# RWKV6 attention and a tanh-shrink layer on one core: the first layer's products joined by three feature tiles instead of two

## The chip, the cores and the metric

The kernel runs on one core of a Trainium2 chip. Four engines matter: TensorE (PE, with its weight loads as PEld), VectorE (DVE), ScalarE (ACT) and SyncE (SP), which issues the transfers from and to device memory. The metric is the time of one execution on the device in microseconds (us). Everything is float32 at the interface; the products of the two layers are made in float32.

## The reference

```python
def _attn_ref(r, k, v, w, u):
    B, H, S, D = r.shape                      # 4, 8, 768, 48
    state = np.zeros((B, H, D, D))
    for t in range(S):
        cur = np.einsum('bhd,bhe->bhde', u[None] * kt, vt)
        y[:, :, t] = np.einsum('bhd,bhde->bhe', rt, state + cur)
        state = wt[:, :, :, None] * state + np.einsum('bhd,bhe->bhde', kt, vt)
...
x = attn_out.transpose(0, 2, 1, 3).reshape(B * S, H * D)   # 3072 x 384
h = x @ w_in                                               # w_in 384 x 2048
g = h - np.tanh(h)
return g @ w_out                                           # w_out 2048 x 384
```

A recurrent attention over 768 steps for 4 batches and 8 heads, whose result, as 3072 tokens of 384 features, goes through two dense layers with g = h - tanh(h) between them.

## The kernel before, in words

**Blocks.** The 3072 tokens are cut into 8 blocks of NB = 384 tokens (a batch's first or second half). For a block the first layer makes 16 feature tiles, each of 128 features by 384 tokens; w_in lies in on-chip memory as `w_in_sb[:, f, k]`, 16 by 3 squares of 128x128. While the two layers of block i run, the attention of block i+1 is worked on piece by piece, and what can be prepared of block i+2. The names of these pieces in code: `earlier` (scores between chunks, products at L508, masked into place by VectorE at L516), `split` and `join` (ScalarE's copies at L556 and L566 that prepare a transposition by DMA, `turned`), `update` (new states: products L589, VectorE's chain L601), `results` (products L785, ScalarE's copies L757 into the next block's tokens `xT`), `bound` (ScalarE's sums over 780 columns, L474). VectorE's own share of them is called `times_behind`, `before`, `held`, `product_u` and the like.

**The first layer.** A tile that stands alone takes three products of 384 columns (`first`, L899), added up in the PSUM bank `hp`. In blocks 2 to 7 some tiles are taken two at a time instead (class `Twos`, from L909): the tokens are cut in two halves of HB = 192, and of the 12 half-size products that two tiles need, a fast matrix product (Winograd's form of Strassen's) leaves 11. It needs sums and differences of squares of w_in (`weight_forms`, L937, made once by VectorE and kept in `kept`), of halves of the tokens (`token_forms`, L945, four per block), and of the results (`begin`): ScalarE copies one product from PSUM to `joint` (L962), and VectorE adds the other six PSUM regions to it in four instructions (L971). Products that only have to be added are added by TensorE in PSUM. Which tiles are joined stands in `JOINED` (L125): three pairs in block 2, six in blocks 3 to 6, seven in block 7; the other tiles stand alone.

**Between the layers.** `slight` (L977) makes g of a tile: two Tanh of different scale on ScalarE (L987, L988), a Square with an accumulated sum (L991) by which the kernel later sees whether the approximation held, and on VectorE the product of the two times a constant (L905).

**The second layer.** `Fewer` takes two tiles of g at a time as 128x128 squares and makes 15 products for 18 (`product`, L1096, 128 columns each) after a fast product too. Its forms of w_out are made in block 1 (L1354), its forms of g by VectorE for every pair (`form_g`, L1010), its 15 running sums over the eight pairs lie in four PSUM regions; products 12 to 14 (`others`, L1124) have a region at times that is shared with the first layer's `hp` or the attention's scratch. At a block's end ScalarE scales the sums out of PSUM (L1109) and VectorE combines them (L1132) into the output.

**The order.** All of it is written in the order in which each engine is to run it. The main loop goes over tiles f of a block; `plan(i)` says which attention piece stands at which tile; the long chain of `if joined ... elif` decides in which order VectorE's instructions of one tile stand, and `between(a, b)` deals two lists alternately, so that an instruction seldom stands directly behind the one whose result it needs. `due` holds second-layer products until two tiles later. PSUM has eight banks: three of `acc`, `hp`, and two pairs of scratch (`att`), which pairs of tiles, attention products and transpositions share in turn. Idle instructions (`empty`) are put in at some blocks' starts to shift code.

## Time and profile before

| | |
|---|---|
| median of 3 runs | 536.88 us (536.12, 536.88, 1406.05) |
| the profiled execution | 535.64 us |
| its span (first to last instruction) | 533.9 us |
| granted TensorE clock, mean | 0.999 |
| instructions | 14969 |
| read from device memory / written | 44.73 MB / 4.72 MB |

The span is what the trace covers; the time of the execution is a little longer. Busy time is the time in which an engine executes. On VectorE and ScalarE the next instruction starts a little before the one ahead has ended, so a row's duration is more than the distance between two starts. A matrix product in float32 shows as two records in the trace. One block of blocks 2 to 6 takes some 62 us.

### The profile page before, as it was taken

The page shows a single profiled execution, that of the slowest core. Times are in us where ns is not written, and L with a number is a line of the kernel's source. Part 1 is how long each engine was busy: PE and PEld are TensorE (multiplying, and loading weights), DVE is VectorE, ACT ScalarE, POOL GpSimd, SP SyncE. Part 2 cuts the span into 40 slices and gives each one's busy share as a digit, 9 for nine tenths or more (in the row PEclk, how much of TensorE's full clock was granted, in tenths as well). Part 3 has the DMA queues.
Part 4 walks back from the last instruction along what each step waited for, and adds up shares of the span by engine and source line. Part 5 has one row for each costly group of instructions (what it writes and reads, how often), then busy time and mean ns, then how long its engine had stood idle before and what let it go on. Part 6 is the DMA issues. An engine that isn't in the chain of part 4 may idle for free.

```text
span 533.9 us, 14969 instructions
## 1 busy us (share of the span) xinstructions
PE 523.9 (98%) x6040; PEld 449.2 (84%) x6040; DVE 478.1 (90%) x1011; ACT 312.4 (59%) x729; POOL 9.1 (2%) x57
## 2 busy tenths in 40 slices
PE   7999999999999999999999999999999999999996
PEld 5756665677887879999799998999889997999994
DVE  7999996698889999999999999999999999667874
ACT  4999984665536473655646375375735655454350
POOL 1100000000000000000000000000000000000001
PEclk9999999999999999999999999999999999999999
DMA  8799632352312452035420832145321430200011
GB/s 282 258 406 342 224 120 71 107 132 64 122 26 72 104 143 95 0 89 166 120 58 2 192 119 66 54 66 142 108 88 31 79 116 1 58 1 1 10 36 48
DMA packets 53048, 56.35 MB, mean 106 GB/s; under 512 B 21488, under 2 KB 50928, under 8 KB 52976
## 3 DMA queue, kind: packets, MB, share of 16 engines
q1 hardware_dynamic: 52592, 55.18, 34.7%
q8 instruction: 49, 0.80, 0.6%
q14 instruction: 23, 0.19, 0.1%
q10 hardware_dynamic: 288, 0.10, 0.1%
q0 software_dynamic: 96, 0.07, 0.1%
HBM read 44.73 MB, written 4.72 MB: 93 GB/s over the span
## 4 chain that ended last, share of the span: by engine, by line
PE 83%; DVE 13%; issue 2%; DMA 1%; SPq 0%; DVEq 0%
PE acc L1096 23%; PE att L961 20%; PE hp L899 17%; PE acc L1047 6%; PE hp L1096 5%; PE att L785 3%; DVE g L1010 2%; PE att L508 2%; DVE joint L971 2%; DVE g L905 1%; PE att L589 1%; DVE pre L431 1%; PE acc L1074 1%; PE att L1096 1%; PE att L899 1%
## 5 line engine op out<-in xcount | busy, mean ns | idle before, releaser
L1096 PE MATMUL acc<-forms,g 128*128 128x128 f32 x972 | 135.5, 276 | 0.0
L1096 PEld LDWEIGHTS acc<-forms,g 128*128 128x128 f32 x972 | 124.3, 192 | 3.8
L899 PE MATMUL hp<-xT,w_sb 128*128 128x384 f32 x330 | 116.5, 489 | 0.0
L1010 DVE TENSOR_TENSOR g<-g 128x256 f32<-128x256 f32 x270 | 110.5, 418 | 6.1 <-DVE g L1010 0.5
L899 PEld LDWEIGHTS hp<-xT,w_sb 128*128 128x128 f32 x330 | 59.5, 190 | 33.3
L905 DVE SCALAR_TENSOR_TENSOR g<-h,qa 128x384 f32<-128x384 f32 x112 | 61.7, 551 | 18.1 <-ACT h L991 17.9
L987 ACT ACTIVATE h<-joint 128x384 f32<-128x384 f32 x54 | 27.9, 517 | 77.5 <-DVE joint L971 77.5
L961 PE MATMUL att<-xT,w_sb 128*128 128x192 f32 x340 | 72.0, 326 | 0.0
L987 ACT ACTIVATE h<-hp 128x384 f32<-128x384 f32 x55 | 27.2, 495 | 58.5 <-PE hp L899 58.4
L991 ACT ACTIVATE h<-h 128x384 f32<-128x384 f32 x113 | 58.2, 515 | 0.0
L961 PEld LDWEIGHTS att<-xT,w_sb 128*128 128x128 f32 x340 | 56.4, 190 | 0.0
L971 DVE TENSOR_TENSOR joint<-joint,att 128x384 f32<-128x384 f32 (+1 forms) x108 | 51.6, 499 | 4.9 <-PE att L961 3.0
L1096 PE MATMUL acc<-w_sb,g 128*128 128x128 f32 x324 | 54.5, 277 | 0.0
L1096 PEld LDWEIGHTS acc<-w_sb,g 128*128 128x128 f32 x324 | 45.9, 192 | 4.4
L961 PE MATMUL att<-turned,kept 128*128 128x192 f32 x192 | 36.5, 327 | 0.1
L1132 DVE TENSOR_TENSOR sums<-sums 128x256 f32<-128x256 f32 x84 | 33.3, 410 | 1.4 <-ACT sums L1109 0.9
L1047 PE MATMUL acc<-w_sb,sums 128*128 128x384 f32 x96 | 33.7, 487 | 0.0
L272 ACT ACTIVATE up<-raw 128x768 f16<-128x768 f32 (+1 forms) x32 | 33.0, 1108 | 0.0
L961 PEld LDWEIGHTS att<-turned,kept 128*128 128x128 f32 x192 | 32.0, 190 | 0.4 <-DVE turned L945 0.4
L1096 PE MATMUL hp<-w_sb,g 128*128 128x128 f32 x176 | 29.5, 275 | 0.0
L1047 PEld LDWEIGHTS acc<-w_sb,sums 128*128 128x128 f32 x96 | 18.1, 190 | 12.3
L988 ACT ACTIVATE qa<-joint 128x384 f32<-128x384 f32 x54 | 27.5, 509 | 0.0
(157 smaller groups left out, 795.5 us busy)
## 6 DMA issues: line engine op xcount, KB each, us to landing
raw<-in_weights SPq DMA_DIRECT2D x16, 768.0 KB, 7.4
w<-in_wT SPq DMA_DIRECT2D x7, 780.0 KB, 4.4
k<-in_kT SPq DMA_DIRECT2D x7, 768.0 KB, 4.6
r<-in_rT SPq DMA_DIRECT2D x7, 768.0 KB, 4.5
v_sb<-in_v SPq DMA_DIRECT2D x8, 576.0 KB, 5.1
k<-in_tokens SPq DMA_DIRECT2D x7, 576.0 KB, 4.1
r<-in_tokens SPq DMA_DIRECT2D x7, 576.0 KB, 4.2
out_y<-sums SPq DMA_DIRECT2D x18, 128.0 KB, 1.9
```

Source lines behind the costliest of these rows:

```text
L272: return lambda: nc.scalar.activation(out=to, in_=of, func=AF.Copy, scale=scale, bias=bias)
L899: nc.tensor.matmul(hp, lhsT=w_in_sb[:, f, kc, :], rhs=xT[kc], start=(kc == KC - 1), stop=(kc == 0))
L905: return lambda: nc.vector.scalar_tensor_tensor(out=out, in0=in0, scalar=scalar, in1=in1, op0=op0, op1=ALU.mult)
L961: nc.tensor.matmul(to, lhsT=lhs, rhs=rhs, start=n == 0, stop=n + 1 == len(of))
L971: return [lambda of=of: nc.vector.tensor_tensor(out=of[0], in0=of[1], in1=of[2], op=ALU.add) for of in ((h[:, 0:5:4], twice(h[:, 3]), both ...
L987: made = nc.scalar.activation(out=t, in_=h, func=AF.Tanh, scale=INNER / UPSCALE)
L988: nc.scalar.activation(out=by, in_=h, func=AF.Tanh, scale=OUTER / UPSCALE)
L991: nc.scalar.activation(out=t, in_=t, func=AF.Square, accum_out=top[:, n:n + 1])
L1010: return lambda: nc.vector.tensor_tensor(out=G[:, to:to + 2], in0=two(G, g_at(q, a0), g_at(q, a1)), in1=two(G, g_at(q, b0), g_at(q, b1)), ...
L1047: nc.tensor.matmul(acc, lhsT=g[:, j * P:(j + 1) * P], rhs=w_out_sb[:, f, :], start=(f == self.first), stop=(f == NF - 1))
L1096: nc.tensor.matmul(to, lhsT=G[:, g_at(q, a), :], rhs=rhs, start=start, stop=stop, skip_group_check=True)
L1132: ops.append(lambda op=op, at=at: nc.vector.tensor_tensor(out=at[0], in0=at[1], in1=at[2], op=OPS[op]))
```

## The change

Blocks 2 to 7 no longer join pairs of tiles but triples. A 3x3 by 3x2 product of blocks (three tiles, three thirds of the features, two halves of the tokens) needs 18 products of 192 columns; the new class `Threes` makes it with 15. A block has five triples, of tiles 0, 3, 6, 10 and 13, and tile 9 alone; block 7 joins four and takes 9, 13, 14, 15 alone.

- **Weight forms.** Eleven sums and differences of w_in's squares per triple. VectorE makes them in block 0 (three triples in one instruction each, 17 instructions) and block 1 (two triples, 17), SP stores them to device memory (`forms_of_w_in`, five times 720 KB), and for each triple SP fetches them back in three parts (192, 256 and 256 KB) into one buffer of 704 KB, `ring`, part of the tile `area`.
- **Token forms.** Ten halves instead of four, in six instructions.
- **Running sums.** Sums over products of one triple stay in PSUM as far as they can: ScalarE takes such a sum off (a "tap", with scale -1, five of them), into `area` or back into another PSUM bank, where TensorE adds further products on it. Six VectorE instructions combine at the triple's end; the results lie in `area`, which has room for one triple.
- **The order.** The three tiles of a triple go through ScalarE during the next triple: `slot` puts one of them between each two stages of products, in front of the tap that stands there. The attention's pieces, the forms of g and the second layer's products are dealt out by hand in `period(t, V, A, fills, tail)`: V is VectorE's list at each of four places, A ScalarE's and TensorE's pieces there, `fills` and `tail` TensorE's.
- **PSUM.** The two scratch pairs become four single banks, used by the triples and by the attention in turn. Masked writes go by bank (four of 384 columns for two of 768), state products are copied to `states` by ScalarE before VectorE works on them there, results go by bank in eight copies instead of four. Products 12 to 14 of the second layer gather in `hp` over the whole block.
- **g's constant** moves from the product (L905) to the scale of the output copies.

The core of the diff:

```diff
-TWOS = range(7)
-BESIDE = (0, 1, 2, 3, 4, 7)
-EMPTY = (159, 0, 92, 0, 16, 0, 40, 0)
-JOINED = {2: (1, 4, 7), 3: BESIDE, 4: BESIDE, 5: BESIDE, 6: BESIDE, 7: TWOS}
+TRIPLES, LONE = (0, 3, 6, 10, 13), 9
+JOINED = 2
+RING = (5, 12, 11, 8, 14, 13, 10, 7, 9, 4, 6)
+RINGS = (0, 3), (3, 7), (7, 11)
+EMPTY = (160, 0, 115, 0, 0, 0, 0, 0)
...
-    class Twos:
...
+    class Threes:
...
+        def load(self, t, part):
+            a, b = (x * P for x in RINGS[part])
+            return nc.sync.dma_start(out=self.ring[:, a:b], in_=drawn[t, :, a:b])
...
+            every = ((y[:, 0:2], a[:, 1:2].to_broadcast([P, 2, HB]), a[:, 0:3:2], "sub"),
+                     (y[:, 2:4], y[:, 0:2], b[:, 1:2].to_broadcast([P, 2, HB]), "add"),
+                     (y[:, 4:6], y[:, 2:4], b[:, 0:3:2], "sub"), (y[:, 6:8], b[:, 2::-2], y[:, 4:6], "sub"),
+                     (y[:, 8], a[:, 2], y[:, 3], "add"), (y[:, 9], y[:, 0], y[:, 6], "add"))
...
+        def begin(self, banks, f0, between, fill):
...
+            def tap(out, of):
+                nc.scalar.activation(out=out, in_=of, func=AF.Copy, scale=-1.0)
...
+            products((3, sums[0]), (5, sums[1]), start=3)
+            between(0)
+            tap(both(1), both(0, True))
+            products((0, singles[0]), (12, singles[1]), start=0)
+            fill(0)
+            products((2, chain[0]), (11, chain[1]))
+            between(1)
+            tap(T[:, 3:7:3], both(1))
+            products((8, sums[0]), (14, sums[1]), (13, apart_sums[0]), start=13)
+            fill(1)
+            products((10, chain[0]), (7, chain[1]))
+            between(2)
+            tap(T[:, 5], apart_sums[0])
+            tap(T[:, 0:5:4], both(1))
+            products((9, apart_sums[1]), (4, apart_sums[0]))
+            fill(2)
+            products((6, chain[0]), (1, chain[1]))
+            tap(T[:, 1:3], both(1))
+            between(3)
+            adding(T[:, 4:7], T[:, 1:4], T[:, 4:7], "add")
+            adding(T[:, 1], singles[0], T[:, 1], "sub")
+            adding(T[:, 0:3:2], both(0), T[:, 0:3:2], "add")
+            adding(T[:, 4:7:2], both(2), T[:, 4:7:2], "sub")
+            adding(T[:, 5], T[:, 5], T[:, 1], "sub")
+            adding(T[:, 1], singles[1], T[:, 1], "add")
...
-        return g, made, square, [product(g, t, RATIO, by, ALU.mult)]
+        return g, made, square, [lambda: nc.vector.tensor_tensor(out=g, in0=t, in1=by, op=ALU.mult)]
...
+        def tail_2(made):
+            load(after, "k", made)
+            last.store()
+            pull(12)
+            if later:
+                ps_a.n = 0
+                later.update_1(ps_a)
+                later.update_out()
+            pull(6)
...
+        h = first(blk.xT, LONE, banks[1][:, 0:NB])
+        chain = later.update_2(True) if later else []
+        waiting.insert(0, (i, LONE, h))
+        made, ops = slot(0)
+        run(form(fewer, 2, 1) + chain[:2] + ops)
+        pull(6)
+
+        def tail_3(made):
+            load(after, "r", made)
+            pull(6)
+            odd(fewer, 2)
+            if later:
+                ps_a.n = 0
+                later.together(ps_a, None)
+                later.result_by_bank()
+                later.fill_holes([nc.sync])
...
+        period(4, [form(fewer, 4, 0), of(after, "behind 0", "take_whole 0") + form(fewer, 4, 1), of(after, "before 2"),
+                   form(fewer, 5, 0) + threes.token_forms(later.x)],
+               [[], [lambda: after and after.bound(HALVES[0])], [lambda: after and after.bound(HALVES[1])], []],
+               [[], [], [lambda: odd(fewer, 3)]], tail_4)
```

In the built programs the instructions stand as follows; each row is a line of the kernel, an operation, output<-inputs and the shape, and in brackets whom it waits for. On VectorE at the end of a pair before (`joint` is the pair's result, att_127 and att_128 are the two scratch pairs of PSUM):

```order
L905 SCALAR_TENSOR_TENSOR g<-h,qa 128x384 [waits Activation_49]
L971 TENSOR_TENSOR joint<-joint,att_128 128x2x192 [waits Activation_49]
L1010 TENSOR_TENSOR g<-g 128x256 [waits DVE_49]
L971 TENSOR_TENSOR joint<-joint,att_127 128x2x192 [waits DVE_49,PE_49]
L971 TENSOR_TENSOR joint<-joint,att_127 128x192 [waits DVE_49]
L971 TENSOR_TENSOR joint<-joint,att_127 128x384
```

And at the end of the first triple of block 3 now (att_598 to att_601 are the four banks):

```order
L1098 TENSOR_TENSOR g<-h,qa 128x384 [waits Activation_49]
L1050 TENSOR_TENSOR area<-area 128x576 [waits Activation_49]
L1050 TENSOR_TENSOR area<-att_601,area 128x192 [waits DVE_49,PE_49]
L1050 TENSOR_TENSOR area<-att_598,area 128x2x192 [waits PE_49]
L1050 TENSOR_TENSOR area<-att_600,area 128x2x192 [waits PE_49]
L1050 TENSOR_TENSOR area<-area 128x192 [waits DVE_49]
L1050 TENSOR_TENSOR area<-att_601,area 128x192 [waits DVE_49]
L1112 TENSOR_TENSOR g<-g 128x256
L1112 TENSOR_TENSOR g<-g 128x256 [waits DVE_49]
```

Six instructions stand for four, the first waits for ScalarE's last tap, and two forms of g behind them stand back to back.

On ScalarE, a pair before: the copy of one product, then a tile of the pair as soon as VectorE has added.

```order
L962 COPY joint<-att_128 128x192 [waits PE_49,Activation_49]
L987 ACTIVATE h<-joint 128x384 [waits DVE_49]
L988 ACTIVATE qa<-joint 128x384
L991 ACTIVATE h,top<-h 128x384 [waits Activation_49]
L987 ACTIVATE h<-joint 128x384 [waits DVE_49]
L988 ACTIVATE qa<-joint 128x384
L991 ACTIVATE h,top<-h 128x384 [waits Activation_49]
```

And one triple now:

```order
L1088 ACTIVATE h<-area 128x384 [waits DVE_49,Activation_49]
L1088 ACTIVATE qa<-area 128x384
L1093 ACTIVATE h,top<-h 128x384 [waits Activation_49]
L1047 ACTIVATE att_599<-att_598 128x384 [waits DVE_49,PE_49]
L1088 ACTIVATE h<-area 128x384
...
L1047 ACTIVATE area<-att_599 128x2x192 [waits PE_49,Activation_49]
...
L1047 ACTIVATE area<-att_600 128x192 [waits DVE_49,PE_49,Activation_49]
L1047 ACTIVATE area<-att_599 128x2x192 [waits PE_49]
L1047 ACTIVATE area<-att_599 128x384 [waits PE_49]
```

The taps L1047 stand in one queue with the three tiles of the triple before, one tile ahead of each of the first three stages.

On TensorE, the middle of a triple now, where products wait for the taps and for the fetched forms:

```order
L1028 MATMUL att_599<-area,w_sb 128x192 [waits Activation_49]
L1028 MATMUL att_599<-area 128x192
L1028 MATMUL att_598<-xT,area 128x192 [waits DMAHW6_49]
L1028 MATMUL att_598<-xT,area 128x192
L1028 MATMUL att_600<-xT,area 128x192
...
L1028 MATMUL att_599<-area 128x192 [waits Activation_49]
L1028 MATMUL att_599<-area 128x192 [waits DMAHW7_49]
L1028 MATMUL att_600<-xT,area 128x192 [waits Activation_49]
L1028 MATMUL att_600<-area 128x192
```

Between these stand the second layer's products (left out); before, the 11 products of a pair stood in one piece with one wait for ScalarE and one for VectorE.

More of the change, by code (lines that the diff above doesn't have):

```diff
@@ L1458 @@
                 op()
-            if outs:
-                add_due(now)
-                if f in (0, 2) and summed and 0 in JOINED[i]:
-                    summed[0].others(ps_a, (4,) if not f else (5, 6, 7), hp)
-                g, made, square, later_ops = slight(twos.h[0], now, i, f)
             rest, behind, formed, forming, held_back = later_ops, [], [], held_back, []
```

590 lines of the change are left out of this document (363 added, 227 removed).

## The prediction

> **What bounds the kernel now.** I read the page's first part, then the busy time by block, then the chain of waits, then VectorE's groups and waits. Busy time of the span (us, share, instructions):
>
> ```profile
> PE 523.9 (98%) x6040; PEld 449.2 (84%) x6040; DVE 478.1 (90%) x1011; ACT 312.4 (59%) x729; POOL 9.1 (2%) x57
> ```
>
> The same by stretch: start:end, length, then busy PE, PEld, DVE, ACT, POOL, granted clock. The last six rows are blocks 2 to 7, cut where VectorE begins their token forms; the first four are pieces of the time before.
>
> ```profile
> 0.00:22.00 22.00, 18.03 (x542) 14.11 (x542) 18.39 (x30) 14.98 (x22) 4.50 (x23) 1.00 0.73 248
> 80.00:93.00 13.00, 13.00 (x42) 7.64 (x41) 9.23 (x15) 5.98 (x18) 0.00 (x0) 1.00 0.25 73
> 93.00:107.00 14.00, 14.00 (x60) 9.33 (x59) 9.66 (x21) 9.16 (x24) 0.00 (x0) 1.00 0.32 108
> ...
> 152.50:214.20 61.70, 61.12 (x726) 52.91 (x726) 57.92 (x131) 32.31 (x81) 0.32 (x4) 1.00 0.34 94
> 214.20:276.50 62.30, 61.50 (x754) 56.99 (x753) 60.11 (x129) 35.61 (x92) 0.32 (x4) 1.00 0.32 90
> 276.50:339.20 62.70, 62.70 (x767) 58.61 (x766) 60.36 (x130) 35.75 (x92) 0.32 (x4) 1.00 0.36 93
> 339.20:401.50 62.30, 62.30 (x766) 58.26 (x765) 60.11 (x129) 35.73 (x92) 0.32 (x4) 1.00 0.37 93
> 401.50:463.90 62.40, 62.40 (x766) 58.41 (x766) 56.71 (x129) 33.80 (x88) 0.18 (x2) 1.00 0.23 54
> 463.90:533.90 70.00, 65.32 (x456) 60.76 (x454) 50.26 (x128) 29.30 (x82) 2.17 (x6) 0.99 0.07 21
> ```
>
> TensorE is full, but in blocks 3 to 5 VectorE is too: 60 of 62 us. In the whole stretch 276.5 to 401.5 (two blocks) its waits for others are these:
>
> ```profile
> DVE joint L971 <- PE att L961: 0.8, 3, 0.3
> DVE g L1010 <- DVE g L1010: 0.5, 1, 0.5
> DVE scores L516 <- PE att L508: 0.2, 1, 0.2
> ```
>
> So the kernel has two bounds at once there: what VectorE is given more than the 2 us that it has free lengthens a block, whatever TensorE saves.
>
> **TensorE's saving.** The chain of waits (start, us, what; two records make a product) gives a half-size product 3.58/11 = 0.325 us, a full one 1.94/3 = 0.645, one of the second layer 2.68/12 = 0.223:
>
> ```profile
> 318.39 1.43 PE att L589 x80
> 321.35 1.94 PE hp L899 x6
> ...
> 327.90 2.83 PE att L785 x192
> ...
> 337.78 2.68 PE acc L1096 x24
> 340.46 3.58 PE att L961 x22
> ```
>
> A full block (3 to 6) has six pairs and four plain tiles: 6 x 3.58 + 4 x 1.94 = 29.2 us. Five triples of 15 products and one plain tile: 75 x 0.325 + 1.94 = 26.3. That is 2.9 us less per block. Over all, the programs hold 57 full products less and 61 half ones more: 36.8 - 19.8 = 17 us off TensorE.
>
> **VectorE's bill.** Its groups in those two blocks (count, busy us, mean ns) and three pieces of its timeline:
>
> ```profile
> L1010 DVE TENSOR_TENSOR g<-g 128x256 f32<-128x256 f32 x80 | 33.1, 418 | 2.0 <-DVE g L1010 0.5
> L971 DVE TENSOR_TENSOR joint<-joint,att 128x384 f32<-128x384 f32 x37 | 20.2, 547 | 0.8 <-PE att L961 0.8
> L516 DVE COPY_PREDICATED scores<-mask_all,att 128x768 f32<-128x768 uint8 x4 | 3.9, 1032 | 0.3 <-PE att L508 0.2
> L1124 DVE SCALAR_TENSOR_TENSOR sums<-hp,outward 128x384 f32<-128x384 f32 x2 | 1.1, 551 | 0.0
> ```
> ```profile
> 344.92 0.55 DVE L971 TENSOR_TENSOR joint<-joint,att 128x384 f32<-128x384 f32 x1
> 345.39 0.42 DVE L1010 TENSOR_TENSOR g<-g 128x256 f32<-128x256 f32 x1
> 345.72 1.40 DVE L971 TENSOR_TENSOR joint<-joint,att 128x384 f32<-128x384 f32 x3
> ...
> 364.51 1.48 DVE L1010 TENSOR_TENSOR g<-g 128x256 f32<-128x256 f32 x3
> 365.91 0.55 DVE L905 SCALAR_TENSOR_TENSOR g<-h,qa 128x384 f32<-128x384 f32 x1
> ...
> 386.91 0.35 DVE L601 TENSOR_TENSOR states<-states,att 128x192 f32<-128x192 f32 x1
> 387.30 0.36 DVE L601 TENSOR_TENSOR states<-states,whole 128x192 f32<-128x192 f32 x1
> ```
>
> From start to start an instruction costs its duration less 0.08 where the next is independent: 0.47 us for 384 columns, 0.34 for 256, 0.27 for 192. Where the next needs its result it costs more: 0.39 for 192 (386.91 to 387.30), 0.47 for 256 (three in 1.40), so 0.12 on top.
>
> Removed per full block: 6 x (3 x 0.467 + 0.27) = 10.0 of additions, 1.1 of token forms (4 x 0.27), 0.5 of L1124. Added: each triple ends in six additions, of 576 columns (0.67, between the rows for 384 and 768), two of 384 and three of 192, three of them with a wait of some 0.1 (by the 0.12 above): 2.7 us, five times 13.5; six token forms, four of 384 and two of 192, nearly each on the one before: 2.9; the masked writes as four of half the width, 0.1. That is 4.9 us more. G's forms, sums and combinations also stand back to back more often (54 dependent neighbours in a block for 30, most of the new ones in the two terms above or at 0.12): 1.6 more. Costed the same way the block before adds up to 61.4, which is its 62.3; the block after to **67.9**. The 29 us of new weight forms fall to blocks 0 and 1 as 17 instructions of 384 columns and 17 of 256, some 13 us. TensorE is full there and VectorE idle for 8 of the 27 us from 80 to 107, and for about 19 us of all 152; I count them hidden, and up to 4 us if they are not.
>
> **The closed loop.** In the change the three tiles of a triple go through ScalarE between the products of the next triple, in one queue with the taps that carry a PSUM sum on, and they read the one `area` that the additions have just written. So additions, three tiles, taps, products and the next additions form a ring, of which no two turns overlap. Behind additions that wait, VectorE holds the next forms of G and the attention's steps, and TensorE waits for those forms. ScalarE's prices, and the step from TensorE to ScalarE (last product ends about 388.83, tanh 389.03: 0.2):
>
> ```profile
> 346.69 0.53 ACT L987 ACTIVATE h<-joint 128x384 f32<-128x384 f32 x1 [4.52 <-DVE joint L971]
> 347.12 0.51 ACT L988 ACTIVATE qa<-joint 128x384 f32<-128x384 f32 x1
> ...
> 348.04 0.51 ACT L987 ACTIVATE h<-joint 128x384 f32<-128x384 f32 x1
> ...
> 350.05 2.94 ACT L556 COPY w<-post 128x768 uint16<-128x768 uint16 x3
> ...
> 370.43 0.75 ACT L566 COPY ks<-ks 128x512 uint16<-128x512 uint16 x1
> 371.05 0.51 ACT L987 ACTIVATE h<-joint 128x384 f32<-128x384 f32 x1
> ...
> 383.91 0.95 ACT L474 ACTIVATE outward<-w,shift 128x780 bf16<-128x780 f32 x1
> ```
> ```profile
> 388.83 1.05 PE L1096 MATMUL acc<-forms,g 128*128 128x128 f32 x8
> 389.03 0.49 ACT L987 ACTIVATE h<-hp 128x384 f32<-128x384 f32 x1 [1.90 <-PE hp L899]
> ```
>
> A tile takes 1.35 us (346.69 to 348.04). No row shows a tap; I take a copy of 384 columns at 0.40 and of 192 at 0.25 (tanh's pitch 0.42; the bounds are 0.3 and 0.6 us, 2 us per block either way). The ring: 0.2, tile 1.35, tap 0.4, tile 1.35, tap 0.4, tile 1.35, short tap 0.25, step 0.2, products 9 and 4 0.65, five products of the second layer 1.1, products 6 and 1 0.65, step 0.2, tap 0.4, step 0.2, additions 2.7: **11.4 us**. Five make 57, less than TensorE's 59.4; but four of the five carry more, since the attention's products use the same four banks and its copies the same queue (VectorE's figure is the 67.9 from above, split at the ends of the additions):
>
> - triple 0: three copies of the splits (2.9 us) beside and in it, 14.5 to 15. VectorE has the token forms and the scans there, 16.7, and decides.
> - triple 1: the scores' products come first, and the banks are free only after the masked writes (four of about 0.5, one bank each); past the first tile's 1.35 that leaves some 1.1: 12.5 (VectorE 11.5).
> - triple 2: two joins (0.62 each, 370.43 to 371.05) and two copies of the sums, some 1.0: 13.6 (VectorE 13.4).
> - triple 3: state products 1.43, four copies, plain tile 9 and its 1.35 before the first slot; with overlap 5.3: 16.7 (VectorE 13.1).
> - triple 4: result products 2.83, eight copies behind them about 2.2, and two sums over 780 columns of 0.95 us each in the queue, 7.1: 18.5 (VectorE 13.2).
>
> Each triple lasts as long as the longer of the two: 16.7 + 12.5 + 13.6 + 16.7 + 18.5 = **78.0 us** for a block of 62.4. If triples 3 and 4 hide all that I put in series it is 69.1; if each of a ring's eight waits costs 0.1 more it is 81.
>
> One rule bears on the ring's PSUM steps. The order has product 9 wait for the tap of product 13, which lies in the other half of its bank. The Trainium skill, PSUM — Partial Sum Buffer, section "PSUM bank collisions raise a hardware error ⚠️", says to guard by bank and quadrant, not by address, since two engines in one bank collide at different addresses too. By that rule the wait cannot go; by address alone a ring would be about 0.33 us shorter, some 10 us over 29 triples, and the time about 604. No run here shows it.
>
> **The sum.** Blocks 3, 4, 5: 15.7 + 15.3 + 15.7 = 46.7. Block 2 has no such triple 0 (VectorE's sum is 3.3 less, the ring then decides with 14.8): 76.1 - 61.7 = +14.4. Block 6 lacks the two sums over 780: 76.1 - 62.4 = +13.7. Block 7 has four triples without attention work, and VectorE gets 6 us more in a block that leaves it 20 us free: +2. The head: 0. The span grows by 76.8, from 533.9 to 610.7. The profiled execution took 535.64, 1.7 more than its span; the median is 1.2 above that one: 613.7, so **614 us**.
>
> **The rivals.**
>
> *VectorE's sum alone decides* (0.22). If the attention's steps hide in the ring, a block lasts its sum and the 0.9 of before: +3.8, +6.5, +6.5, +6.5, +1.0 for blocks 2 to 6, +2 for block 7: **563 us**. For it: VectorE is gapless now, and the order puts up to 12 second-layer products behind the additions. Against it: copies and tiles stand in one queue, and `area` is single.
>
> *TensorE stays the bound* (0.03), the other side: its 17 us come off and VectorE's additions hide: **520 us**. It decides only if VectorE gets through a block in 59.4 us; it is busy for 60.1 now, and the counts give it 4.9 more.
>
> *The forms come late* (0.05). A triple's 704 KB arrive in three parts into a single buffer. The nearest rows:
>
> ```profile
> raw<-in_weights SPq DMA_DIRECT2D x16, 768.0 KB, 7.4
> k<-in_tokens SPq DMA_DIRECT2D x7, 576.0 KB, 4.1
> ```
>
> The last part (256 KB) is freed by the last product but one and read again some 6 us later. At the first row's 7.4 it is 1.4 late in each of 29 triples: **655 us**. Against it: at the second row's 4.1 it is in time, and the DMA engines are busy for a third. SP issues these 15 transfers a block in order with its others; behind the parts for triple 1 stand the tokens of k, which VectorE takes up some 4 us after the additions of triple 0.
>
> *The clock falls in TensorE's new waits* (0.05). Products of the ring take about 2 us on its path; doubled in half the triples, 30 us: **644 us**. Against it: 18.03 busy of 22 us at the start kept 1.00. The Trainium skill, TensorE: Matmul & The Clock Gate, section "HAM oscillation — how this bites in real kernels", wants no idle gap over about 3.4 us; the ring leaves TensorE idle for some 18 us in 78, in five turns of several waits each, so by it the clock should hold.
>
> **How the numbers follow.** The ring as forecast has 0.60; inside it the overlap in triples 3 and 4 and the taps' price give 590 to 636 (half of the 8.9 us per block that series or overlap makes, up or down). With the rivals 0.95 is told; 0.05 is for a lesser mix of ring and VectorE, 565 to 590. Eight in ten: 556 to 640, which leaves out the 520, the 644 and the 655. About 2% (10.7 us) is what a measurement can tell from no change: faster than 526 only in the second rival, 0.03; within 2%, if VectorE's dependent neighbours cost nothing and everything else hides, 0.04; slower 0.93.
>
> **What would show it.** Right: TensorE's busy time down by some 17 us, its share to 82 to 86%; VectorE's busy time up by 25 to 30 us; gaps on VectorE before the last additions of a triple that end on ScalarE's tap, largest in triples 3 and 4; blocks of 74 to 81 us, unequal triples in them. Wrong: VectorE gapless with blocks of 69 (first rival); waits of products on the DMA queue (third); blocks under 62.

## The result, and the profile after

The change takes 2765.6 us (median of 4 runs, 2764.23 to 2766.42), the kernel before 537.16 in the same comparison: 5.15 times as long, 95% interval 5.14 to 5.16. One run of the kernel before, of 1406.05 us, is left out of this ratio as a slow one. The forecast was 614 us with a range to 640. The direction was forecast; the size was not, by a factor that no rival on record reaches.

The first two rows of the page after, span and busy time:

```profile
span 2764.7 us, 35425 instructions
...
PE 1601.1 (58%) x14464; PEld 1104.8 (40%) x14464; DVE 1073.4 (39%) x2288; ACT 870.5 (31%) x1919; POOL 13.6 (0%) x85
```

The number of instructions is the first sign: 35425 where there were 14969, and 14464 of TensorE's where there were 6040. The change by itself adds some 400 (15366 in the run with three faults mended, below). So code ran that had not run before. VectorE's timeline shows where it begins:

```profile
658.23 0.55 DVE L1098 TENSOR_TENSOR g<-h,qa 128x384 f32<-128x384 f32 x1
660.06 0.15 DVE L1794 TENSOR_SCALAR again<-att 1x1 int32<-1x1 f32 x1 [1.28 <-PE att L1793]
660.14 4.99 DVE L1253 TENSOR_TENSOR sums<-sums 128x256 f32<-128x256 f32 x12
665.66 1.47 DVE L1180 SCALAR_TENSOR_TENSOR g<-acc,g 128x384 f32<-128x384 f32 x3 [0.53 <-POOL g L1264]
667.05 0.35 DVE L1180 SCALAR_TENSOR_TENSOR g<-att,g 128x192 f32<-128x192 f32 x1
681.58 1.00 DVE L533 COPY_PREDICATED scores<-mask_all,att 128x768 f32<-128x768 uint8 x1 [14.18 <-PE att L518]
```

At 660 us `again` is written (L1794), the last output sums are finished at 667.4, and then the attention's scores are made anew. `again` is the kernel's own guard: it counts flags, one for each decay, each bound and each tile's sum of squares (L1093, compared with LIMIT), and where one is missing the whole problem is worked out a second time by general code, block after block with little overlap (the branch `anew` at the end of both kernels): in the last row below TensorE, VectorE and ScalarE are busy for 997 of 1000 us between the three of them. The busy time by stretch; the first two rows are blocks 3 and 4 of the first pass, the others the second pass:

```profile
238.98:325.43 86.45, 69.00 (x766) 63.75 (x764) 65.54 (x138) 45.18 (x119) 0.32 (x4) 0.92 0.40 109
325.43:410.90 85.47, 68.06 (x766) 63.10 (x764) 65.97 (x138) 44.93 (x118) 0.32 (x4) 0.92 0.41 110
...
700.00:1000.00 300.00, 149.69 (x1623) 95.36 (x1622) 83.58 (x199) 70.22 (x145) 0.36 (x4) 0.67 0.06 19
1000.00:2000.00 1000.00, 495.15 (x3492) 289.76 (x3492) 258.62 (x548) 242.97 (x495) 0.53 (x6) 0.71 0.07 22
```

So there are two questions. Why does the guard trip? And why do blocks 3 to 5 of the first pass take 85 to 87 us, where the forecast has 78 and the kernel before 62?

### The profile page after: what moved, and what is told of

The parts are those of the page before. It is cut to its first block, busy times and chain, and to the rows that moved or that the text cites. A ratio compares the mean times of both kernels' runs of the same rounds, so it can differ in the third digit from the quotient of the medians.

```text
span 2764.7 us, 35425 instructions
## 1 busy us (share of the span) xinstructions
PE 1601.1 (58%) x14464; PEld 1104.8 (40%) x14464; DVE 1073.4 (39%) x2288; ACT 870.5 (31%) x1919; POOL 13.6 (0%) x85
## 4 chain that ended last, share of the span: by engine, by line
PE 48%; DVE 23%; ACT 17%; DMA 5%; issue 4%; SPq 2%; DVEq 0%; POOL 0%; ACTq 0%; POOLq 0%
PE acc L1149 19%; PE hp L952 12%; DVE h L958 5%; PE att L518 5%; PE att L1028 3%; PE acc L1198 3%; DVE sums L1130 3%; DVE th L1126 3%; DVE sums L958 3%; ACT qa L1122 3%; ACT h L1121 2%; ACT qb L1123 2%; ACT h L1117 2%; PE att L835 2%; DVE area L1050 2%
## 5 line engine op out<-in xcount | busy, mean ns | idle before, releaser
L1149 PE MATMUL acc<-w_sb,sums 128*128 128x384 f32 x864 | 538.7, 788 | 744.7 <-DVE sums L1130 744.7
L1149 PEld LDWEIGHTS acc<-w_sb,sums 128*128 128x128 f32 x864 | 251.6, 309 | 995.1 <-DVE sums L1130 827.0
L952 PE MATMUL hp<-xT,w_sb 128*128 128x384 f32 x930 | 381.0, 551 | 31.4 <-DMA xT<-outward 31.4
L952 PEld LDWEIGHTS hp<-xT,w_sb 128*128 128x128 f32 x930 | 207.8, 227 | 200.7 <-issue 91.3
L518 PE MATMUL att<-pre,post 48*64 48x32 f32 (+1 forms) x4608 | 134.6, 280 | 149.3 <-DVE pre L903 106.5
L518 PEld LDWEIGHTS att<-pre,post 48*64 48x64 f32 x4608 | 124.5, 205 | 161.2 <-issue 110.7
L1028 PE MATMUL att<-area 128*128 128x192 f32 x348 | 85.7, 343 | 1.0 <-ACT area L1047 1.0
L1130 DVE COPY_PREDICATED sums<-big,th 128x384 f32<-128x384 int32 x128 | 75.2, 588 | 13.6 <-DVE sums L958 0.5
L1122 ACT ACTIVATE qa<-h,shift 128x384 f32<-128x384 f32 x128 | 78.6, 614 | 4.2
L1047 ACT ACTIVATE area<-att 128x384 f32<-128x384 f32 x116 | 49.0, 445 | 97.8 <-PE att L1028 97.8
L1125 ACT ACTIVATE big<-h,shift 128x384 f32<-128x384 f32 x128 | 76.6, 599 | 0.0
```

The costliest lines, as they stand in the source:

```text
L518: self.done = nc.tensor.matmul(dst, lhsT=self.chunk(lhs, p, 2 * c + par)[rows], rhs=src, start=(h, par) not in begun, stop=True, skip_grou ...
L952: nc.tensor.matmul(hp, lhsT=w_in_sb[:, f, kc, :], rhs=xT[kc], start=(kc == KC - 1), stop=(kc == 0))
L1028: nc.tensor.matmul(to, lhsT=lhs, rhs=rhs, start=start, stop=True, skip_group_check=True)
L1122: nc.scalar.activation(out=qa, in_=s, func=AF.Square, bias=shift[:, 0:1])
L1125: nc.scalar.activation(out=big, in_=s, func=AF.Relu, bias=shift[:, 2:3])
L1130: nc.vector.copy_predicated(out=g, mask=big.bitcast(I32), data=th)
```

## The experiments

### The guard and the second pass

Reading the change with the trace beside it gave the suspicion. TensorE's products on raw tokens (not on forms) wait 21 us over the run for transfers into `xT`, and a single fifth triple waits 4.5 us so; the first row is the group's on the page, the second from the waits of the fifth triple of block 2:

```profile
L1028 PE MATMUL att<-xT,area 128*128 128x192 f32 x290 | 73.1, 371 | 39.8 <-DMA xT<-outward 21.4
...
PEld att L1028 <- DMA xT<-outward: 4.5, 1, 4.5
```

These transfers fill the *next* block's tokens. A product of the present block has no reason to wait for them. The list of VectorE's work that `period(4, ...)` is given holds `threes.token_forms(later.x)`; Python builds that list before `period` issues the triple's products, and `token_forms` sets `self.raw` to the next block's tokens while it is being called, not when its instructions stand. So the fifth triple multiplies raw halves of the next block and forms of its own.

**Its own tokens.**

```diff
-            self.raw, y = x, self.x
+            y = self.x
...
+        threes.raw = blk.x        # at the head of each block
```

> One assignment is moved, so that the fifth triple's products read the tokens of their own block; nothing else changes. Theory A (the list for the fifth triple is built before its products are issued, and building it already points the products at the next block's tokens; the results are too large, the kernel's own guard on the size of h trips, and the whole second pass runs): no second pass, and the fifth triple no longer waits for the next block's transposed tokens. In the trace of the change the first pass ends at about 667 us, with fifth triples of 24 to 25.6 us; at the forecast 18.5 each it ends at 667 - 5 x 6.6 = 634, a time of about 636 us. Rival B (the guard trips for another reason, such as sums kept in PSUM or flags added up too early): the second pass stays, about 2730 us.

Measured: 668.13 us (667.38 to 671.66), 1.247 [1.242, 1.251] times the kernel before. The second pass is gone, and so is the wait for the transfers; the same group now:

```profile
L1028 PE MATMUL att<-xT,area 128*128 128x192 f32 x290 | 68.1, 350 | 20.8 <-ACT area L1047 20.5
```

Theory A holds for the guard. Its second half, 636 us, does not: the fifth triple still takes 24.4 to 25.4 us in blocks 2 to 5. (In this run, the next and the one with sums behind the taps, some forms of g are made too early or not at all, as in the change; their time is that of the same instructions on partly other data.)

**The guard's limit.**

```diff
-LIMIT = float(np.tanh(INNER * SLIGHT ** 0.5) ** 2 * (1.0 - 2.0 ** -16))
+LIMIT = 5.0 * float(np.tanh(INNER * SLIGHT ** 0.5) ** 2 * (1.0 - 2.0 ** -16))
```

> The change as it is, but the guard's limit for the sums of squares is five times as high, so that it no longer sees what it is there for. Theory A (squares of tiles 13 to 15 are too large, two to four times those of other tiles): the second pass is not entered and the time is that of the first pass as it stands, 667 + 2 = 669 us. Rival B (one of the other flags trips, on the decay or on its bounds, or their number is wrong): 2765 us, as the change.

Measured: 675.73 us in one run, no second pass. It is the sums of squares that trip the guard, and a limit five times as high lets them through; by how much they exceed the old one no run shows. The time is 7 us above what I read from the trace of the change, most of it because an execution ends some 5 us behind VectorE's last row, which I had taken for its end.

**Both passes of the kernel before.**

```diff
-            nc.vector.tensor_single_scalar(again, sure[0:1, 0, 0:1], float(P * (n_whole + n_excess + n_top)),
+            nc.vector.tensor_single_scalar(again, sure[0:1, 0, 0:1], float(P * (n_whole + n_excess + n_top) + 1),
```

> The kernel before, with the guard's count compared to a number one too high, so that the second pass always runs. If the second pass is the same old code and costs what the trace of the change shows behind 667 us (some 2097 us), this takes 537 + 2097 = 2634 us. If the second pass has itself become slower by the change, less.

Measured: 2623.78 us in one run, 10 less than the 2634 expected. So the second pass costs 2623.8 - 536.9 = 2087 us in the kernel before, and 2765.6 - 675.7 = 2090 in the change. It is old code at its old price; the change only caused it to run.

**Three faults mended.** Two more places in the change are wrong: one list leaves out the last forms of block 1, and the first forms of each block's fourth pair stand ahead of the product of the tile that they read. The guard does not trip on them: with its own tokens alone the second pass no longer ran.

```diff
-    left = rest + formed + forming + behind
+    left = rest + formed + forming + behind + held_back
...
-        period(3, [chain[2:5], form(fewer, 3, 0) + chain[5:8], chain[8:], ...
+        period(3, [chain[2:5], chain[5:8], form(fewer, 3, 0) + chain[8:], ...
```

> As the run with its own tokens, and two more orders mended: the last forms of block 1's eighth pair, which the change never makes, are made (three VectorE instructions, once), and the first forms of a block's fourth pair are made one place later, behind the product of the tile that they read. In the run with its own tokens the sums of blocks 1 to 7 had been made from forms of the wrong data. Theory: these orders cost next to nothing, 668 us within 2. If the later forms hold TensorE up in the fourth triple, up to 1 us in each of six blocks more: 674.

Measured: 663.48 us (663.09 to 665.20), 1.236 [1.234, 1.239]. Not dearer but 4.6 us cheaper than with its own tokens; the fourth triple of block 7 shows 1.6 us of it (13.7 us for 15.3), the fifth of block 2 another 2.0 (23.4 for 25.4). Why is not shown. This is what the change costs when it computes what it is meant to, and the base for the rest. Its blocks 2 to 7:

```profile
155.38:237.68 82.30, 64.75 (x732) 58.63 (x732) 64.14 (x130) 41.31 (x106) 0.32 (x4) 0.94 0.42 114
237.68:323.22 85.54, 69.69 (x764) 64.20 (x764) 65.51 (x138) 45.04 (x119) 0.32 (x4) 0.92 0.41 110
323.22:408.49 85.27, 69.25 (x764) 64.03 (x764) 65.86 (x138) 44.84 (x118) 0.32 (x4) 0.92 0.40 110
408.49:493.84 85.35, 69.44 (x764) 64.15 (x764) 65.52 (x137) 45.07 (x119) 0.32 (x4) 0.92 0.40 110
493.84:572.98 79.14, 66.31 (x764) 61.50 (x764) 60.22 (x132) 42.87 (x114) 0.18 (x2) 0.96 0.35 89
572.98:661.30 88.32, 71.42 (x454) 63.29 (x454) 53.18 (x130) 35.81 (x99) 2.16 (x6) 0.94 0.13 39
```

No engine is full any more, and the clock is below 1. VectorE's work in blocks 3 to 5 is 65.5 to 65.9 us, 5.4 more than before.

### The triples

The additions of 576 columns (L1050) that end a triple divide the time. In the run with three faults mended, VectorE's timeline has those of block 5's five triples and of block 6's first:

```profile
421.75 0.75 DVE L1050 TENSOR_TENSOR area<-area 128x576 f32<-128x576 f32 x1
435.04 0.76 DVE L1050 TENSOR_TENSOR area<-area 128x576 f32<-128x576 f32 x1 [1.76 <-ACT area L1047]
449.01 0.75 DVE L1050 TENSOR_TENSOR area<-area 128x576 f32<-128x576 f32 x1
465.60 0.76 DVE L1050 TENSOR_TENSOR area<-area 128x576 f32<-128x576 f32 x1 [2.63 <-ACT area L1047]
490.32 0.76 DVE L1050 TENSOR_TENSOR area<-area 128x576 f32<-128x576 f32 x1 [6.10 <-ACT area L1047]
507.10 0.75 DVE L1050 TENSOR_TENSOR area<-area 128x576 f32<-128x576 f32 x1
```

From row to row the second to fifth triple take 13.3, 14.0, 16.6 and 24.7 us and the next first one 16.8. The brackets say who was late: nobody in the first and third, where VectorE works almost without a gap; ScalarE's tap in the second, fourth and fifth. For the first to fifth triple 16.7, 12.5, 13.6, 16.7 and 18.5 were forecast, with the same engines in the same places but for the third, which was to be the ring's by 0.2 us. Four are met within 0.8 us; the fifth is 6.2 longer.

**More VectorE work, fourth triple; the same, first triple; more ScalarE work, fourth triple.** Three runs that put known work into one triple of each block:

```diff
+        def idle(n):
+            o = outward[0][:, 0:NB]
+            return [lambda: nc.vector.tensor_tensor(out=o, in0=o, in1=o, op=ALU.max)] * n
...
-        period(3, [chain[2:5], chain[5:8], ...
+        period(3, [chain[2:5], chain[5:8] + idle(5), ...
```
```diff
-            V = [form(last, 5, 1) + of(later, ...
+            V = [form(last, 5, 1) + idle(5) + of(later, ...
```
```diff
+            return [lambda: nc.scalar.copy(out=o, in_=o)] * n
...
-               [[], [], [], []], [[], [], [lambda: odd(fewer, 1)]], tail_3)
+               [[], idle(6), [], []], [[], [], [lambda: odd(fewer, 1)]], tail_3)
```

> As the run with three faults mended, with five idle VectorE instructions of 384 columns (0.58 us each, 2.9 in all) in the fourth triple, where the trace shows 16.4 to 16.6 us and VectorE waiting. Theory ring: they fall into VectorE's waits, no more than 3 us over six blocks. Rival (VectorE's sum of work sets the time): 2.9 us in each of six blocks, 17 us more.

> As the run with three faults mended (663.5 us), with the same five idle VectorE instructions (2.9 us) in the first triple of blocks 3 to 7 instead of the fourth, where they cost some 4 us over six blocks. The first triple takes 16.8 us and its additions begin without a wait. Theory (VectorE's work sets the first triple, the ring the others): 2.9 us in each of four or five blocks, 11 to 15 more, 675 to 679 us. Rival (the ring sets it too): 4 us more at most.

> As the run with three faults mended (663.5 us), with six idle ScalarE copies of 384 columns (0.41 us each from start to start, 2.5 in all) in the fourth triple behind its second tile, ahead of the tap there. ScalarE is busy for little more than half of the time. Theory ring: they lengthen the fourth triple of each block by 2.2 to 2.5 us, 13 to 15 us in all, 677 to 679 us, where more VectorE work at the same place cost 4 us. Rival (ScalarE has the room): 3 us at most.

Measured: 667.60, 679.26 and 693.56 us, so 4.1, 15.8 and 30.1 more than 663.48, where at most 3, 11 to 15 and 13 to 15 were expected. VectorE's 2.9 us lengthen the fourth triple by 0.1 to 0.5, 1.7 us of the 4.1 in all; the rest lies at the head, in block 2 and at the end, and the four runs spread from 664.44 to 669.54. In blocks 3 to 6 they lengthen the first triple by 2.8 and the second behind it by 1.0. The rows from the run with more work in the first triple: block 4's fifth, then block 5's first three:

```profile
411.60 0.76 DVE L1050 TENSOR_TENSOR area<-area 128x576 f32<-128x576 f32 x1 [5.87 <-ACT area L1047]
431.21 0.75 DVE L1050 TENSOR_TENSOR area<-area 128x576 f32<-128x576 f32 x1
445.48 0.76 DVE L1050 TENSOR_TENSOR area<-area 128x576 f32<-128x576 f32 x1 [2.42 <-ACT area L1047]
459.43 0.75 DVE L1050 TENSOR_TENSOR area<-area 128x576 f32<-128x576 f32 x1
```

19.6 us for 16.8. In block 7, whose first triple waits 2.9 us for a tap, the same work adds nothing (16.95 us for 16.96). That is what ring and VectorE, whichever is longer, should do. ScalarE's 2.5 us cost more than themselves: the fourth triple grows by 3.1 to 5.4 us, up to twice the forecast. ScalarE is busy for 55% of the span, and yet what is put ahead of a tap lengthens the triple, since its queue is part of the ring. Why more than 2.5 is in the clock of such a triple, the last two stretches of the fourth triple of block 6 in that run:

```profile
568.00:572.00 4.00, 1.26 (x5) 1.14 (x4) 1.56 (x5) 3.87 (x11) 0.00 (x0) 0.76 0.14 46
572.00:577.77 5.77, 5.77 (x27) 5.44 (x26) 0.56 (x1) 1.27 (x4) 0.00 (x0) 0.58 0.19 50
```

While the tap is late TensorE has 1.26 us of work in 4; the granted clock falls to 0.76 and 0.58. TensorE's first two products behind that tap, in the run with three faults mended and in this one:

```profile
546.12 0.82 PE L1028 MATMUL att<-area 128*128 128x192 f32 x4
...
570.79 1.65 PE L1028 MATMUL att<-area 128*128 128x192 f32 x4 [2.74 <-ACT area L1047]
```

From there to the triple's end it is 4.6 us without the copies and 7.0 with them, so some 2.4 us come on top of the copies' own.

### The fifth triple

Its timeline on ScalarE, in the run with three faults mended:

```profile
478.80 0.23 ACT L1093 ACTIVATION_READ_ACCUMULATOR h<-h 128x1 f32 x1
480.89 0.94 ACT L484 ACTIVATE outward<-w,shift 128x780 bf16<-128x780 f32 x1 [1.86 <-DMA xT<-outward]
481.74 0.19 ACT L484 ACTIVATION_READ_ACCUMULATOR outward<-w,shift 128x1 f32 x1
481.83 0.47 ACT L1047 ACTIVATE area<-att 128x384 f32<-128x384 f32 x1
...
489.80 0.49 ACT L1047 ACTIVATE area<-att 128x384 f32<-128x384 f32 x1 [4.65 <-PE att L1028]
```

The first of the two sums over 780 columns (L484) waits 1.86 us, not for its input but for a transfer out of `outward`: it writes its throw-away output into that buffer, from which SP is filling the holes of the next tokens. The tap stands behind it, TensorE behind the tap. The same triple by stretch shows what that does to TensorE (second column busy PE, near the end the clock):

```profile
465.60:469.50 3.90, 1.04 (x7) 0.85 (x7) 3.69 (x9) 0.00 (x0) 0.00 (x0) 0.94 0.84 269
469.50:473.50 4.00, 4.00 (x132) 3.78 (x135) 2.77 (x5) 0.00 (x0) 0.18 (x2) 0.63 0.00 0
...
481.50:485.50 4.00, 2.04 (x6) 1.53 (x7) 2.50 (x4) 3.65 (x11) 0.00 (x0) 0.65 0.26 74
485.50:490.32 4.82, 4.82 (x25) 4.82 (x24) 0.00 (x0) 0.49 (x1) 0.00 (x0) 0.58 0.05 7
```

Twice it stands for some 2 to 3 us and is then given a clock near 0.6, the second time for the products that the last tap waits for.

**The sums behind the taps** (on the run with its own tokens), **and the same with three faults mended:**

```diff
-               [[], [lambda: after and after.bound(HALVES[0])], [lambda: after and after.bound(HALVES[1])], []],
+               [[], [], [], [lambda n=n: after and after.bound(HALVES[n]) for n in range(2)]],
```

> As the run with its own tokens, with ScalarE's two sums over 780 columns (0.95 us each) of the fifth triple moved from between the tiles to behind the last tap, where the additions of 2.7 us cover them. Theory ring (the closed loop of additions, tiles and taps sets the fifth triple): shorter by up to 1.9 us in each of blocks 2 to 5, some 7 us in all. Rival (VectorE's sum of work sets it): no difference, within 1 us.

> The run with the warm fourth triple (642.0 us) without its five idle products: three faults mended, and the two sums behind the taps. Theory clock: the fourth triple's end halves the clock again, 1 us or less per block by the triples' lengths there (18.1 to 18.7 us with them, 19 without): 644 to 647 us. Rival (the idle products do nothing): 642 us within 1.

Measured: 644.90 us (643.24 to 648.54) for 668.13, and 639.91 (639.24 to 640.86) for 663.48: 23 us both times, three times what the ring theory had put down for it; both forecasts of the second run, 644 to 647 and 642, lie above it. There the fifth triple of blocks 2 to 5 falls to 17.1 to 20.0 us. By the two traces these triples and the first ones behind them make 22 us of the 23.6; the other 1.6 lie in block 6's fifth triple, which holds none of the sums (17.2 us for 18.8). In block 4 of the later run the clock stays at 1.00 all through it:

```profile
371.58:375.50 3.92, 1.06 (x9) 0.87 (x9) 3.71 (x9) 0.00 (x0) 0.00 (x0) 1.00 0.83 261
375.50:379.50 4.00, 4.00 (x201) 3.76 (x201) 2.76 (x5) 0.98 (x5) 0.18 (x2) 1.00 0.03 11
379.50:383.50 4.00, 3.21 (x21) 2.73 (x20) 1.65 (x2) 4.00 (x15) 0.00 (x0) 1.00 0.09 22
383.50:388.76 5.26, 4.75 (x35) 4.46 (x35) 4.79 (x9) 2.87 (x10) 0.00 (x0) 1.00 0.35 102
```

17.2 us, though TensorE stood as long at its beginning (1.06 busy in 3.92) as where the clock fell to 0.63 (1.04 in 3.90).

**The sums written elsewhere.**

```diff
-            junk = outward[1].bitcast(BF16)[:, 0:UP * NCH * LP]
+            junk = outward[0 if i >= 8 else 1].bitcast(BF16)[:, 0:UP * NCH * LP]
```

> As the run with three faults mended, but ScalarE's two sums over 780 columns stay between the tiles and write their throw-away output to another buffer, which no transfer reads. Theory A (they wait 1.9 us for the transfers that fill the next tokens' holes from their buffer, the tap behind them waits, TensorE stands idle and its clock is halved): most of the 5.6 us per block that moving them brought, 4 to 5.5 in each of blocks 2 to 5, so 647 to 652 us. Rival B (the 1.9 us of their own time in the queue and what the clock makes of it is what counts): a gain of 2 us or less per block, 660 us or more.

Measured: 651.30 us (650.58 to 653.76). The sums wait for nothing any more. The fifth triple takes 20.5 to 22.0 us for 23.4 to 24.9, the next first triple 0.9 more; 12.2 us in all. That is inside the time forecast by theory A, at its upper end, but 3 us per block, less than the 4 to 5.5 it names. So of the 23.6 us that the two sums cost where they stand, 12 are the wait for the transfer with what follows from it, and the other 11 their own time in the queue with what follows from that (7.6 us would be that time alone, four blocks of 1.9).

**A warm fourth triple's end.**

```diff
         def tail_3(made):
             load(after, "r", made)
+            for _ in range(5):
+                nc.tensor.matmul(banks[1][:, 0:NB], lhsT=w_in_sb[:, LONE, 0], rhs=blk.xT[0], start=True, stop=True)
```

> As the run with three faults mended, with the two sums moved behind the taps (645 us where that was done alone) and, at the fourth triple's end, five products of 384 columns whose result nobody reads, 3.2 us, where TensorE stands idle while VectorE adds. Theory clock (that idle time of nearly 4 us halves the granted clock, 0.69 in the 4 us behind it, and the state's products and others then take twice as long): the clock stays at 1.00 there, and each of six blocks saves about 1.5 to 2 us: 634 to 638 us. Rival (the clock falls for another reason, or the products behind it wait for VectorE's forms anyway): 645 us or up to 3 more.

Measured: 642.02 us (640.82 to 642.94), against 639.91 without the idle products. The clock does stay at 1.00 through these fifth triples. In blocks 2 and 3, where without the idle products it fell to a mean of 0.83 and 0.91, they bring 1.8 and 0.6 us (18.1 us for 20.0, 18.3 for 19.0); in blocks 4 to 6 the clock held anyway, and there they stand ahead of the attention's results and cost 1.0 to 2.4. So the theory is right on the clock and wrong on the gain: 2 us are lost, little more than the runs of either kernel spread. Of the idle times tried, the one behind a late tap costs most. In the run with three faults mended TensorE also stands up to 3.9 us at the head of a first triple, waiting for token forms, and the clock is 0.90 over block 5's first triple; yet that triple has the length that VectorE's work gives it.

### The end of block 7

**The last tiles earlier** (on the warm run):

```diff
+    run(shrink())
+    *checked, product_of = shrink()
+    run(checked)
     pull(12)
     odd(fewer, 5)
     second.added(12, gs[12])
-    run(shrink())
...
-    for op in rest:
+    for op in rest + sums_of:
```

> As the run with the warm fourth triple (642.0 us), with the end of block 7 in another order: tiles 14 and 15 go through ScalarE ahead of the copies that take the second layer's sums out of PSUM, and VectorE makes the output's 12 sums ahead of the guard's result instead of behind it. Theory (of the 18 us that block 7's end is longer than before, VectorE's 5 us of sums at the very end are a part that nothing covers): 3 to 5 us less, 637 to 639 us. Rival (TensorE's debt, 24 us of products behind the last triple, decides alone): no difference within 1.5 us.

Measured: 638.91 us (636.71 to 639.45), 3.1 less than 642.02. The time is as the theory had it, but the run moves two things, and the traces give the gain to the other one: VectorE's last product of g starts 23.3 us behind the last triple's additions without the change of order and 20.1 with it, where the tiles come earlier; from there to the end it is 14.3 and 13.6 us. By this the sums bring some 0.6 us, not 3 to 5: made earlier, they leave VectorE waiting for TensorE's last products. The theory's number came true by luck; no run moves one of the two alone. What else makes the end long is seen in the stretch behind the last triple of the run with three faults mended:

```profile
624.70:630.00 5.30, 2.44 (x21) 2.25 (x21) 4.74 (x11) 2.40 (x7) 0.00 (x0) 1.00 0.00 2
630.00:636.00 6.00, 6.00 (x37) 4.67 (x36) 4.67 (x11) 1.71 (x6) 0.00 (x0) 1.00 0.01 3
636.00:652.50 16.50, 15.95 (x89) 11.72 (x87) 6.85 (x21) 4.86 (x12) 0.00 (x0) 1.00 0.01 1
652.50:661.30 8.80, 0.00 (x0) 0.00 (x0) 3.04 (x8) 0.00 (x0) 2.16 (x6) 0.74 0.21 70
```

36.6 us: TensorE owes 24 us of products when the last triple is done, and then 8.8 us pass without it.

## Why the prediction was wrong, point by point

- **The step that failed: "The sum".** It adds up one pass over the blocks, each instruction at its price whatever numbers it works on, and puts the guard's second pass at nothing, without a reason. The second pass is in the code of both kernels, and the forced run prices it at 2087 us; the list that trips the guard stands in the change. The cause is shown: moving one assignment removes the second pass, and so does a higher limit for the squares. 2090 of the 2152 us above the forecast are this.
- **The sizes that failed besides: triple 4 (the fifth) and block 7.** In the mended run they are what carries the time out of the range; the points below have their terms.
- **TensorE's 17 us off: not seen.** The products were saved, as 57 full and 61 half ones are counted in the programs; but TensorE's busy time rose from 523.9 to 559.4 us in the mended run, 52 more than forecast. The clock makes at most some 36 of it (an estimate: 1 - 0.945 of the span of 661.3 us). The other 16 are there at a better clock as well: with the sums moved TensorE is busy for 549.4 us, 42 more than forecast, at most 26 of them by the clock. A product that starts behind a wait shows a longer row (0.59 us for 0.49 at 192 columns, at 547.45 and 547.88 in the mended run), which may be it; no run isolates it. So the sign "82 to 86%" came true, at 85%, by luck: 559 of 661 us, where 507 of 611 were forecast.
- **VectorE's bill: right for a block.** 4.9 us more work were forecast, 5.4 are measured in blocks 3 to 5. The sign of 25 to 30 us over the span holds for blocks 2 to 7 alone (28.9); with the new weight forms at the head it is 40.5, from 478.1 to 518.6.
- **The ring: right in form, and in four of five triples in size.** 16.7, 12.5, 13.6, 16.7 against 16.8, 13.3, 14.0, 16.6; who waits for whom is as forecast but for the third, which VectorE sets, and the three runs with added work bear out which engine sets the first and the fourth. The clock is 1.00 in the second to fourth triple of block 5, so these meet the forecast on its own terms; the fourth rests on an overlap that was guessed, and its 0.1 us of error is in part luck.
- **"two sums over 780 columns of 0.95 us each in the queue": mis-sized.** 1.9 us were put down; moving them gains some 22 us over four blocks, 5.5 each. I had costed their time and not looked at what they write: the buffer is also the source of the transfers that the new order of results puts just ahead of them. Missing were the 1.86 us of wait, and the clock, which falls behind a late tap and lengthens the ring's products. Without the sums 16.6 us were forecast for this triple; 17.1 to 20.0 are measured.
- **The clock: too little.** The rival "the clock falls in TensorE's new waits" had 0.05 and 30 us. It is no rival but a part of the ring: mean clock 0.945 in the mended run, 0.959 with the sums moved.
- **Block 7, +2: mis-sized.** It takes 88.3 us for 70.0, +18.3. The argument was that VectorE has 20 us free there. But the four rings take 51.7 us by themselves, and the three plain tiles, TensorE's 24 us of products and the sums come behind them; I had not added up the block by the ring that the rest of the prediction rests on.
- **The forms from device memory: hidden, as forecast.** 256 KB land in 2.7 us, and no product waits for them in the waits of the mended run's blocks 3 to 6. (A triple's forms are 704 KB, stored as they are fetched; the 720 KB named with the change are the same amount counted in thousands of bytes.)
- **VectorE alone (563), TensorE alone (520): both excluded** by the runs with added work: VectorE's 2.9 us add next to nothing to the fourth triple, and ScalarE's copies lengthen it though TensorE is given no work.

For the mended change the sum reads, against the forecast span of 610.7: head +2.9 (within the up to 4 named for weight forms that are not hidden), block 2 +6.2, blocks 3 to 5 +22.2, block 6 +3.0, block 7 +16.3, together 661.3. Even without the second pass it lies above the range's 640. The fastest version run takes 638.9 us, 1.189 [1.186, 1.192] times the kernel before; it still holds the idle products, which cost some 2 us, and no run points to a version that beats the kernel before.

## What to carry to other kernels

Where a kernel holds a guard with a general path behind it, a change to what is computed has to be read for what it computes before its time is forecast; the count of executed instructions shows at once which path ran. When code builds its lists of instructions ahead of issuing them, look for what is set while the list is built. And in a closed ring over three engines, the price of an instruction is not its duration: ask what its output buffer waits for, and what TensorE's clock does while the ring stands.

## What the runs showed of the hardware that was not expected

TensorE's clock is given up after shorter pauses than I had thought, and not the same way each time. TensorE's timeline in the run with the sums moved and three faults mended, the beginning of block 3's fifth triple and then of block 4's; two records are one product of 128 columns:

```profile
294.52 0.81 PE L1198 MATMUL acc<-forms,g 128*128 128x128 f32 x4 [2.86 <-DVE g L1112]
295.12 0.64 PE L1198 MATMUL hp<-w_sb,g 128*128 128x128 f32 x2
...
374.77 0.71 PE L1198 MATMUL acc<-forms,g 128*128 128x128 f32 x4 [2.86 <-DVE g L1112]
375.32 0.39 PE L1198 MATMUL hp<-w_sb,g 128*128 128x128 f32 x2
```

The same instructions behind the same pause of 2.86 us: in the first block a product behind it takes 0.64 us, in the second 0.39, and the triples take 18.97 and 17.18. In the run with three faults mended a pause of 2.50 us behind a late tap was enough, after 4 us at a clock of 1.00:

```profile
482.35 1.36 PE L1028 MATMUL att<-area 128*128 128x192 f32 x4 [2.50 <-ACT area L1047]
```

Two products of 192 columns take 1.36 us there, for 0.82 in the row of the same two without a wait above. The Trainium skill, TensorE: Matmul & The Clock Gate, section "What's actually happening", says that the window by which the clock is set runs freely and is not reset when a kernel starts; the two outcomes behind one length of pause agree with that. Its section "HAM oscillation — how this bites in real kernels" puts the harmful idle gap at more than about 3.4 us, which the prediction set against the rival of a falling clock; the gaps of 2.50 and 2.86 us here speak against that figure as a safe bound.
